# Loading x in two pairs of tiles, with both halves of the value weights between them

## The chip, the cores and the metric

The kernel runs on one core of one Trainium2 chip. The metric is the device time of one execution in microseconds (us), and the median of several executions is compared. The core has five engines that run side by side: TensorE (PE, matmuls; PEld is its weight load), VectorE (DVE), ScalarE (ACT), GpSimd (POOL) and SyncE (SP). Here SP does nothing but issue transfers from the chip's main memory into on-chip memory and back.

## The reference

The inputs are a sequence x of 2048 rows by 512, and weights, all in bfloat16. Two branches are computed from x and mixed row by row with a gate:

```
g = sigmoid((x * gate_w).sum(-1))
q, k, v = x @ wqkv, in 32 heads of 16
pq, pk = q @ w_phi, k @ w_phi               # per head
phi_q = [softmax(pq), softmax(-pq)];  phi_k likewise
kv = phi_k^T v;  z = sum of phi_k           # over all rows, per head
o = (phi_q kv) / (phi_q z + 1e-6);  a = o @ wo
b = relu(x @ w1) @ w2                        # inner width 1376
out = g * a + (1 - g) * b
```

## The kernel before

The 2048 rows are 16 tiles of 128, and four chunks of 512. On chip the kernel needs x with its columns on the partitions (`XT`), as the operand of every product with x. Chunks 1 to 3 come through transposing loads. The first chunk, tiles 0 to 3, is loaded as it is into part of the buffer `FT` and turned by TensorE: `xt{m}a` and `xt{m}b` are two matmuls each against an identity (line 321), for the first and second half of the columns of tile m. ScalarE copies the first half from the accumulator memory (PSUM) to `XT` (`xe{m}0`, line 333), VectorE the second (`xe{m}1`, line 335). "The turns" are these transposes.

Of the first chunk come then the value products `v{m}a`, `v{m}b` (line 369): two matmuls each of 128x512, with the first and second half of the value weights `WV`; ScalarE evicts the four-matmul result (`ve{m}`, line 374). The hidden units `h{c}_{k}` (line 392, four matmuls for chunk c and 128 of the inner columns) are evicted with a relu (`rl{c}_{k}`). The folds `f1_{j}` (line 351) multiply w_phi into the key weights, so that one product of x (`pr_k...`, line 449) gives pk; they need the key weights through the transposing load `wkT`, and are evicted as `fe1_{j}`, by VectorE for even j and ScalarE for odd j. All the rest of the kernel (softmax features, kv, the output products) comes behind.

PSUM has eight banks. The lines below give the transposes' banks, per tile for first and second half, and the folds' banks; the value tiles 0 to 3 accumulate in banks 2, 3, 4, 5 (`VB`), and the hidden units turn through 3, 4, 5 (`HB`):

```
XB, FB = ((0, 1), (6, 7), (0, 1), (6, 7)), (6, 7, 0, 1)
VB = (2, 3, 4, 5)
HB = (3, 4, 5)
```

The order of each engine's work is written out by name in the table `ORDER`, one list per engine, and each engine goes through its list in order. A task waits on semaphores for the tasks named in its dependencies; a load counts as done when it has landed whole. The numbers `dur` and `lat` in the source are a planner's costs and are not used when `ORDER` is given. SP's list starts with xa (three tiles of x, 384 KB), wva and wvb (the halves of the value weights, 256 KB each), xb (the fourth tile, 128 KB), then w1a (the first part of w1), wphi and wkT. In xa each partition holds three consecutive rows, so tile m of 0 to 2 holds rows 3p + m, and the function `rows` sends the output tiles back in the same manner.

While the first load is under way TensorE runs `warm0`, matmuls of constants whose result is not used (line 251).

Of the kernel before, what the change touches and what calls it, by code (L numbers as in the profile page):

```python
# [15 lines left out]

ORDER = {
    "sp": (
        "xa wva xb wvb w1a wphi wkT w1b x1 gw w1c wqT x2 x3 w2a ht0 w2b ht1 wo ht3 tq0 tq1 tq2 tq3 to0 to1 tq4 "
        "tq5 to2 to3 tq6 tq7 to4 ht2 to5 tq9 tq8 to6 to7 tq10 tq11 to8 to9 tq12 tq13 to10 to11 tq14 tq15 to12 "  # L20
        "to13 to14 to15 st15_1 "
    ),
# [6 lines left out]
    ),  # L29
    "act": (  # L30
# [20 lines left out]
    ),  # L51
# [29 lines left out]
class _Graph:  # L81
# [6 lines left out]
    def add(self, name, eng, fn, deps=(), dur=0.1, lat=None, dma=False):  # L88
        assert name not in self.tasks, name
        found = []  # L90
        for d in deps:
            if d is None:
                continue
            t = self.tasks[d]
            if t not in found:
                found.append(t)
        self.tasks[name] = _Task(name, eng, fn, found, dur, self.LAT[eng] if lat is None else lat, dma)
        return name
# [44 lines left out]
def bass_gated_mix__linear_kernel_hedgehog__dense_activation_relu__prompt_kernel(  # L143
# [11 lines left out]
    x2 = A_x.rearrange("b s d -> (b s) d")  # L155
    o2 = out.rearrange("b s d -> (b s) d")
    S, D = x2.shape
    H, DH = A_w_phi.shape[0], A_w_phi.shape[1]
    DFF = B_w1.shape[1]
    P = 128  # L160
# [13 lines left out]
    NPB, NTS, NF, NSL = 3, 3, 4, 3  # L174
# [6 lines left out]
    with ExitStack() as es:  # L181
        E = es.enter_context

        def sb(name, shape, dt):
            return E(nc.sbuf_tensor(name, shape, dt))
# [5 lines left out]
        WV = sb("WV", [P, ND, D], BF16)  # L191
# [8 lines left out]
        FT = sb("FT", [P, NF, 2 * F], BF16)  # L200
# [35 lines left out]
        add = g.add  # L236
# [12 lines left out]
        def pe_warm(q, sizes):  # L249
            for n in sizes:  # L250
                last = q.matmul(PS[:, 5, 0:n], ONE[:, 0:P], ONE[:, 0:n], start=True, stop=True)
            return last

        add("warm0", "pe", lambda q: pe_warm(q, (D, D, D, D, D, D, P, 2 * P)), (), dur=1.46)

        queue = {}

        def after_last(name, eng):
            if eng in queue:
                g.follow(queue[eng], name)  # L260
            queue[eng] = name

        def load(name, eng, out_, in_, deps=(), dur=0.1, lat=6.0, **how):
            add(name, eng, lambda q: q.dma_start(out=out_, in_=in_, **how), deps, dur=dur, lat=lat, dma=True)
            after_last(name, eng)
# [7 lines left out]

        w1r = B_w1.rearrange("(j p) n -> p j n", p=P)
        wvr = A_wqkv[:, 2 * D:3 * D].rearrange("(j p) n -> p j n", p=P)
        load("xa", "sp", FT[:, NF - 2, 0:3 * D], x2[0:3 * P, :].rearrange("(p t) d -> p (t d)", t=3), dur=0.47, lat=2.6)
        load("wva", "sp", WV[:, 0:2, :], wvr[:, 0:2, :], dur=0.47, lat=3.3)
        load("xb", "sp", FT[:, NF - 2, 3 * D:4 * D], x2[3 * P:4 * P, :], dur=0.47, lat=4.2)
        load("wvb", "sp", WV[:, 2:4, :], wvr[:, 2:4, :], dur=0.49, lat=3.8)
        load("w1a", "sp", W1[:, :, 0:512], w1r[:, :, 0:512], dur=0.5, lat=4.9)  # L280
        load("wphi", "sp", WPS[:, :, :], A_w_phi.rearrange("(g hl) r c -> (hl r) g c", g=ND), dur=0.55, lat=4.7)
        load_t("wkT", WT[:, ND:2 * ND, :], A_wqkv[:, D:2 * D], (), 4.55, 2.0)
# [25 lines left out]
        wbd = [f"wbd{j}" for j in range(ND)]  # L308


        def evict(name, eng, out_, b, deps):
            if eng == "act":
                add(name, eng, lambda q: q.activation(out_, PS[:, b, :], ACT.Copy), deps, dur=0.6)
            else:
                add(name, eng, lambda q: q.tensor_copy(out_, PS[:, b, :]), deps, dur=0.69)

        XB, FB = ((0, 1), (6, 7), (0, 1), (6, 7)), (6, 7, 0, 1)

        def pe_xt(q, m, n):
            for j in (2 * n, 2 * n + 1):  # L320
                last = q.matmul(PS[:, XB[m][n], (j % 2) * P:(j % 2 + 1) * P], XN[:, m, j * P:(j + 1) * P],  # L321
                                IDN[:, :], start=True, stop=True)
            return last

        for m in range(4):
            for n in range(2):
                add(f"xt{m}{'ab'[n]}", "pe", lambda q, m=m, n=n: pe_xt(q, m, n),
                    ("xa" if m < 3 else "xb", "ident", f"xe{m - 2}{n}" if m > 1 else None), dur=0.11)
            for n, eng in enumerate(("act", "dve")):
                xo = XT[:, 2 * n:2 * n + 2, m * P:(m + 1) * P]  # L330
                xi = PS[:, XB[m][n], 0:2 * P].rearrange("p (j t) -> p j t", j=2)
                if eng == "act":
                    add(f"xe{m}{n}", eng, lambda q, o=xo, i=xi: q.activation(o, i, ACT.Copy), (f"xt{m}a",), dur=0.38)
                else:
                    add(f"xe{m}{n}", eng, lambda q, o=xo, i=xi: q.tensor_copy(o, i), (f"xt{m}b",), dur=0.42)
# [6 lines left out]
        HB = (3, 4, 5)  # L342

        def rows(m):
            if m < 3:
                return o2[0:3 * P, :].rearrange("(p t) d -> p t d", t=3)[:, m, :]
            return o2[m * P:(m + 1) * P, :]

        def pe_fold(q, s, j, b):
            for i in range(ND):  # L350
                last = q.matmul(PS[:, b, i * P:(i + 1) * P], WT[:, s * ND + i, j * P:(j + 1) * P], WBD[:, i, :],  # L351
                                start=True, stop=True)
            return last

        for j in range(ND):
            b = FB[j]
            add(f"f1_{j}", "pe", lambda q, j=j, b=b: pe_fold(q, 1, j, b), ("wkT", *wbd, f"xe{3 - j // 2}{j % 2}"), dur=0.24)
            evict(f"fe1_{j}", ("dve", "act")[j % 2], WP[:, 1, j, :], b, (f"f1_{j}",))
        units = []
        for c in range(NC):  # L360
# [6 lines left out]
        def pe_v(q, m, js, b):  # L367
            for j in js:
                last = q.matmul(PS[:, b, :], XT[:, j, m * P:(m + 1) * P], WV[:, j, :],  # L369
                                start=(j == 0), stop=(j == ND - 1))  # L370
            return last

        def evict_v(m, b, deps):
            add(f"ve{m}", "act", lambda q: q.activation(  # L374
                ap(VS, NT * NG * GZ, m * NG * GZ, [[GZ, NG], [1, GV]]), psap(b * 512, [[GV, NG], [1, GV]]), ACT.Copy),
                deps, dur=0.6)

        for m in range(4):
            for n, js in enumerate(((0, 1), (2, 3))):
                add(f"v{m}{'ab'[n]}", "pe", lambda q, m=m, js=js: pe_v(q, m, js, VB[m]),  # L380
                    (f"xe{m}{n}", f"wv{'ab'[n]}", *((f"v{m}a",) if n else ())), dur=0.44)
            evict_v(m, VB[m], (f"v{m}b",))
        freed = {b: (f"ve{m}",) for m, b in enumerate(VB)}
        add("gt", "pe", lambda q: q.matmul(PS[:, 2, 0:ND], GWR[:, :], IDN[:, 0:ND], start=True, stop=True),  # L384
# [19 lines left out]
        n = 0  # L404
        for kind, a, k in units:
            b = HB[n % len(HB)]
# [23 lines left out]
        for c in range(NC):  # L430
# [3 lines left out]
                dur=0.2)  # L434
# [3 lines left out]
        for m in range(4, NT):  # L438
            add(f"v{m}", "pe", lambda q, m=m: pe_v(q, m, range(ND), 2), (*xof[m // 4], "wva", "wvb", f"ve{m - 1}" if m > 4 else "gv"),
                dur=0.865)  # L440
# [15 lines left out]
        for jn, (kind, tiles) in enumerate(jobs):  # L456
            w = len(tiles)
            n = kind_n[kind]
# [63 lines left out]
            else:  # L522
# [4 lines left out]
                    dur=0.11 + 0.207 * w)  # L527
# [24 lines left out]
                for m in tiles:  # L552
# [22 lines left out]
                    ab = HB[m % 3]  # L575
# [15 lines left out]
                    if m == NT - 1:  # L591
# [15 lines left out]
                        for h2 in range(2):  # L607
                            b, cs = hb[h2], cols[h2]
# [12 lines left out]
                            else:  # L621
                                add(f"oe{m}_1", "dve", lambda q, m=m, b=b, cs=cs: q.tensor_scalar(  # L622
                                    OSB[:, m % NOS, cs], PS[:, b, 0:cs.stop - cs.start], OMG[:, m:m + 1], None, ALU.mult), need,
                                    dur=0.4)
                            add(f"st{m}_{h2}", ("act", "sp")[h2], lambda q, m=m, cs=cs: q.dma_start(
                                out=o2[m * P:(m + 1) * P, cs], in_=OSB[:, m % NOS, cs]), (f"oe{m}_{h2}",), dur=0.5,
                                lat=1.5, dma=True)
# [5 lines left out]
                        (f"a{m}", f"go{m // 4}", f"st{m - NOS}" if m >= NOS else None), dur=0.69)  # L633
                    add(f"st{m}", "act", lambda q, m=m: q.dma_start(
                        out=rows(m), in_=OSB[:, m % NOS, :]), (f"oe{m}",), dur=0.39, lat=1.7, dma=True)

        for line in (("warm0", "xt0a", "xt0b", "xt1a", "xt1b", "xt2a", "xt2b", "xt3a", "xt3b", "h0_0"),
# [44 lines left out]
```

## Time and profile before

| | |
|---|---|
| median of 3 runs | 150.67 us (150.57 to 150.94) |
| the profiled execution | 150.76 us, of which the span from first to last instruction is 148.9 us |
| TensorE busy | 145.6 us, 98% |
| VectorE, GpSimd, ScalarE busy | 110.8, 109.6, 91.9 us |
| loads and stores | 16.11 MB moved, 108 GB/s in the mean |

The profile's times count from the start of the span. A line of the view in order of time has the start, the length, the engine, the line of the source, the operation, output and inputs, the number of instructions that were merged, and in brackets the idle time of that engine just before, with what ended it. PEld shows when weights are loaded, SPq when SP issues a transfer. The length of matmuls that follow each other includes the way through the array, so the pace is read from the starts.

### The profile page before, as it was taken

Reading aid. Unit: us, or ns where it says so; the run is one execution under the profiler, and the core shown is the slowest. Engines: PE = TensorE matmul, PEld = TensorE weight load, DVE = VectorE, ACT = ScalarE, POOL = GpSimd, SP = SyncE. Lnnn points to the kernel's source line nnn. Section 1 sums busy time; section 2 is a strip of 40 time slices with the busy share of each in tenths; the row PEclk is TensorE's granted clock in tenths of the full one; section 3 lists DMA queues with packets and bytes.
Section 4 is the critical chain, followed back from the end, with each engine's and each line's share of the span. In section 5 each row is a group of like instructions: output and inputs, shape, how many; then the busy total and the mean of one; then the engine's idle time right before and its main releaser. Section 6 shows DMA issues by size and latency. Waiting matters only on the chain.

```text
span 148.9 us, 2554 instructions
## 1 busy us (share of the span) xinstructions
PE 145.6 (98%) x984; PEld 73.6 (49%) x984; DVE 110.8 (74%) x169; ACT 91.9 (62%) x127; POOL 109.6 (74%) x73
## 2 busy tenths in 40 slices
PE   7999999999999999999999999999999999999994
PEld 2445444445446644455455545454545444445453
DVE  0344799999997769894879979799999966618301
ACT  3458679996896897774989591566455651303051
POOL 4000799999999999999999999999999924510000
DMA  4999999600200420000000135954767787864543
GB/s 148 292 179 236 238 176 237 221 0 0 65 1 0 97 88 0 0 0 0 4 2 0 35 70 135 116 135 112 170 48 174 184 206 144 174 146 116 128 151 101
DMA packets 45524, 16.11 MB, mean 108 GB/s; under 512 B 39272, under 2 KB 45384, under 8 KB 45512
## 3 DMA queue, kind: packets, MB, share of 16 engines
q1 hardware_dynamic: 43208, 13.89, 43.9%
q10 hardware_dynamic: 2304, 2.06, 4.3%
q8 instruction: 8, 0.13, 0.4%
q14 instruction: 4, 0.03, 0.1%
HBM read 4.41 MB, written 2.10 MB: 44 GB/s over the span
## 4 chain that ended last, share of the span: by engine, by line
PE 96%; DMA 2%; DVE 0%; issue 0%
PE PS L580 24%; PE PS L392 23%; PE PS L449 19%; PE PS L369 9%; PE PS L586 9%; PE PS L516 3%; PE PS L559 3%; DMA FT<-in_A_x_dram 2%; PE PS L400 2%; PE PS L601 2%; PE PS L351 1%; PE PS L321 1%; PE PS L612 1%; DVE OSB L622 0%; PE PS L384 0%
## 5 line engine op out<-in xcount | busy, mean ns | idle before, releaser
L495 POOL TENSOR_TENSOR TS<-MN,PB 128x1024 bf16<-128x1024 bf16 (+1 forms) x18 | 30.9, 1723 | 13.3 <-DVE MN L488 13.3
L392 PE MATMUL PS<-XT,W 128*128 128x512 bf16 x160 | 38.4, 379 | 0.0
L502 DVE TENSOR_REDUCE ZB<-FT 128x128 f32<-128x2048 bf16 (+1 forms) x18 | 36.5, 2031 | 1.9 <-ACT FT L500 1.8
L580 PE MATMUL PS<-W,HT 128*128 128x512 bf16 (+1 forms) x165 | 37.8, 379 | 0.0
L500 ACT ACTIVATE FT<-TS 128x2048 bf16<-128x2048 bf16 (+1 forms) x18 | 30.9, 1719 | 4.8 <-POOL TS L495 4.2
L495 POOL TENSOR_TENSOR TS<-PB,MX 128x1024 bf16<-128x1024 bf16 (+1 forms) x18 | 30.9, 1720 | 0.0
L449 PE MATMUL PS<-WP,XT 128*128 128x512 bf16 x128 | 30.1, 379 | 0.0
L509 POOL TENSOR_TENSOR FT<-FT,SC 128x2048 bf16<-128x2048 bf16 (+1 forms) x9 | 29.5, 3287 | 0.0
L410 ACT ACTIVATE HT<-PS 128x512 bf16<-128x512 f32 x40 | 22.6, 596 | 4.7 <-PE PS L392 3.9
L631 ACT ACTIVATE OSB<-PS,OMG 128x512 bf16<-128x512 f32 x15 | 10.3, 685 | 24.4 <-PE PS L586 24.3
L580 PEld LDWEIGHTS PS<-W,HT 128*128 128x128 bf16 (+1 forms) x165 | 15.4, 98 | 17.2 <-ACT OSB L631 0.7
L482 ACT ACTIVATE PB<-PS 128x1024 bf16<-128x1024 f32 (+1 forms) x18 | 16.7, 927 | 10.5 <-PE PS L449 5.5
L392 PEld LDWEIGHTS PS<-XT,W 128*128 128x128 bf16 x160 | 14.7, 98 | 16.4 <-ACT HT L410 0.9
L488 DVE TENSOR_REDUCE MN<-PB 128x64 bf16<-128x1024 bf16 (+1 forms) x18 | 19.4, 1090 | 4.4 <-ACT PB L482 4.3
L486 DVE TENSOR_REDUCE MX<-PB 128x64 bf16<-128x1024 bf16 (+1 forms) x18 | 19.4, 1086 | 3.6 <-ACT PB L482 3.6
L449 PEld LDWEIGHTS PS<-WP,XT 128*128 128x128 bf16 x128 | 12.2, 98 | 14.2 <-ACT PB L482 0.5
L369 PE MATMUL PS<-WV,XT 128*128 128x512 bf16 x64 | 16.4, 379 | 0.1
L532 POOL TENSOR_TENSOR FT<-FT,SR 128x1024 bf16<-128x1024 bf16 (+1 forms) x9 | 15.6, 1735 | 0.6
L586 PE MATMUL PS<-WO,OT 128*128 128x512 bf16 x60 | 14.8, 379 | 0.0
L567 DVE SCALAR_TENSOR_TENSOR OTM<-PS,EG,RD 128x256 bf16<-128x256 f32 x32 | 14.3, 467 | 0.2
L565 DVE RECIPROCAL RD<-PS 128x16 f32<-128x16 f32 x32 | 6.7, 234 | 8.8 <-PE PS L559 8.8
L374 ACT ACTIVATE VS<-PS 128x512 bf16<-128x512 f32 x16 | 9.4, 600 | 2.2 <-PE PS L369 2.2
(54 smaller groups left out, 98.2 us busy)
## 6 DMA issues: line engine op xcount, KB each, us to landing
out_dram<-OSB ACTq DMA_DIRECT2D x15, 128.0 KB, 2.2
W<-in_B_w_dram SPq DMA_DIRECT2D x1, 1280.0 KB, 7.3
W<-in_B_w_dram SPq DMA_DIRECT2D x2, 512.0 KB, 5.2
WV<-in_A_wqkv_dram SPq DMA_DIRECT2D x2, 256.0 KB, 4.1
WO<-in_A_wo_dram SPq DMA_DIRECT2D x1, 512.0 KB, 4.0
FT<-in_A_x_dram SPq DMA_DIRECT2D x1, 384.0 KB, 3.3
W<-in_B_w_dram SPq DMA_DIRECT2D x1, 352.0 KB, 3.8
PHQ<-FT SPq DMA_TRANSPOSE x16, 2.8
```

The lines of the kernel that those rows point to most:

```text
L369: last = q.matmul(PS[:, b, :], XT[:, j, m * P:(m + 1) * P], WV[:, j, :], start=(j == 0), stop=(j == ND - 1))
L392: last = q.matmul(PS[:, b, :], W1[:, j, k * P:(k + 1) * P], XT[:, j, chunk(c)], start=(j == 0), stop=(j == ND - 1))
L410: add(f"rl{a}_{k}", "act", lambda q, a=a, k=k, b=b: q.activation(HT[:, k, chunk(a)], PS[:, b, :], ACT.Relu), (f"h{a}_{k}",), dur=0.6)
L449: last = q.matmul(PS[:, pj + n, :], XT[:, j, m * P:(m + 1) * P], WP[:, s, j, :], start=(j == 2), stop=(j == 1))
L486: add(f"mx_{J}", "dve", lambda q, sl=sl, w=w, i=pbg: q.tensor_reduce(MX[:, sl, 0:w * H], i, AX.X, ALU.max), (f"ev_{J}", old("t1")), dur=0. ...
L488: add(f"mn_{J}", "dve", lambda q, sl=sl, w=w, i=pbg: q.tensor_reduce(MN[:, sl, 0:w * H], i, AX.X, ALU.min), (f"ev_{J}", old("t2")), dur=0. ...
L495: add(f"{tn}_{J}", "pool", lambda q, o3=o3, a3=a3, b3=b3: q.tensor_tensor(o3, a3, b3, ALU.subtract), (f"{'mx' if sg == 0 else 'mn'}_{J}", ...
L500: add(f"ex_{J}", "act", lambda q, fs=fs, ts=ts, w=w: q.activation(FT[:, fs, 0:w * F], TS[:, ts, 0:w * F], ACT.Exp), (f"t1_{J}", f"t2_{J}", ...
L502: add(f"sm_{J}", "dve", lambda q, fs=fs, sl=sl, w=w: q.tensor_reduce(ZB[:, sl, 0:2 * w * H], FT[:, fs, 0:w * F].rearrange("p (g d) -> p g ...
L509: add(f"nm_{J}", "pool", lambda q, f3=f3, sl=sl, w=w: q.tensor_tensor(f3, f3, SC[:, sl, 0:2 * w * H].unsqueeze(2).to_broadcast([P, 2 * w * ...
L580: last = q.matmul(PS[:, ab, :], HT[0:r, k, m * P:(m + 1) * P], W2[0:r, k, :], start=(k == 0), stop=False)
L586: last = q.matmul(PS[:, ab, :], OT[:, m % NOT, t, :], WO[:, t, :], start=False, stop=(t == ND - 1))
```

## The change

The first load takes two tiles of x and the second load of x the other two, each 256 KB, with two consecutive rows per partition; both halves of the value weights come between them. TensorE turns tiles 0 and 1, does all the value products of these two, and then turns tiles 2 and 3. Tile 2's transposes use banks 4 and 5, tile 3's banks 0 and 1; dependencies follow the banks. `v3a` waits for `xe21`, which frees bank 5. The warm-up has one matmul of 256 columns less. In ScalarE's list `ve1` comes ahead of `xe20`, and the orders of the first hidden units and folds and of their evictions change a little. The planner's costs in the loads change too.

```diff
 "sp":
-        "xa wva xb wvb w1a wphi wkT w1b x1 gw w1c wqT x2 x3 w2a ht0 w2b ht1 wo ht3 tq0 tq1 tq2 tq3 to0 to1 tq4 "
+        "xa wva wvb xb w1a wphi wkT w1b x1 gw w1c wqT x2 x3 w2a ht0 w2b ht1 wo ht3 tq0 tq1 tq2 tq3 to0 to1 tq4 "
 "act":
-        "xe00 xe10 xe20 xe30 ve2 ve0 ve1 ve3 fe1_3 rl0_1 fe1_1 rl0_0 ev_k0 rl0_2 ev_k1 ev_k2 ex_k0 rl0_3 rl0_5 "
+        "xe00 xe10 ve1 xe20 xe30 ve0 ve2 ve3 fe1_3 fe1_1 rl0_0 rl0_1 ev_k0 rl0_2 ev_k1 ev_k2 ex_k0 rl0_3 rl0_5 "
 "pe":
-        "warm0 xt0a xt0b xt1a xt1b xt2a xt2b v0a v2a v1a xt3a v1b v2b xt3b v0b v3a h0_1 v3b h0_0 f1_3 f1_2 f1_0 "
-        "f1_1 h0_2 pr_k0a pr_k0 pr_k1 pr_k2 pr_k3 h0_3 gt h0_5 h0_6 h0_4 h0_8 h0_9 v4 pr_k4 h1_0 h0_7 h1_1 pr_k5 "
+        "warm0 xt0a xt0b xt1a xt1b v0a v1a v1b v0b xt2a xt2b xt3a xt3b v2a v2b v3a h0_0 h0_1 v3b f1_3 f1_2 f1_1 "
+        "f1_0 h0_2 pr_k0a pr_k0 pr_k1 pr_k2 pr_k3 h0_3 gt h0_5 h0_6 h0_4 h0_8 h0_9 v4 pr_k4 h1_0 h0_7 h1_1 pr_k5 "
...
-        add("warm0", "pe", lambda q: pe_warm(q, (D, D, D, D, D, D, P, 2 * P)), (), dur=1.46)
+        add("warm0", "pe", lambda q: pe_warm(q, (D, D, D, D, D, D, P)), (), dur=1.36)
...
-        load("xa", "sp", FT[:, NF - 2, 0:3 * D], x2[0:3 * P, :].rearrange("(p t) d -> p (t d)", t=3), dur=0.47, lat=2.6)
-        load("wva", "sp", WV[:, 0:2, :], wvr[:, 0:2, :], dur=0.47, lat=3.3)
-        load("xb", "sp", FT[:, NF - 2, 3 * D:4 * D], x2[3 * P:4 * P, :], dur=0.47, lat=4.2)
-        load("wvb", "sp", WV[:, 2:4, :], wvr[:, 2:4, :], dur=0.49, lat=3.8)
+        def pair(i):
+            return x2[2 * i * P:2 * (i + 1) * P, :].rearrange("(p t) d -> p (t d)", t=2)
+
+        load("xa", "sp", FT[:, NF - 2, 0:2 * D], pair(0), dur=0.47, lat=2.35)
+        load("wva", "sp", WV[:, 0:2, :], wvr[:, 0:2, :], dur=0.47, lat=2.65)
+        load("wvb", "sp", WV[:, 2:4, :], wvr[:, 2:4, :], dur=0.48, lat=3.4)
+        load("xb", "sp", FT[:, NF - 2, 2 * D:4 * D], pair(1), dur=0.47, lat=3.9)
...
-        XB, FB = ((0, 1), (6, 7), (0, 1), (6, 7)), (6, 7, 0, 1)
+        XB, FB = ((0, 1), (6, 7), (4, 5), (0, 1)), (6, 7, 0, 1)
...
-                    ("xa" if m < 3 else "xb", "ident", f"xe{m - 2}{n}" if m > 1 else None), dur=0.11)
+                    ("xa" if m < 2 else "xb", "ident", f"xe0{n}" if m > 2 else None), dur=0.11)
...
-            if m < 3:
-                return o2[0:3 * P, :].rearrange("(p t) d -> p t d", t=3)[:, m, :]
+            if m < 4:
+                i = m // 2
+                return o2[2 * i * P:2 * (i + 1) * P, :].rearrange("(p t) d -> p t d", t=2)[:, m % 2, :]
...
-            add(f"f1_{j}", "pe", lambda q, j=j, b=b: pe_fold(q, 1, j, b), ("wkT", *wbd, f"xe{3 - j // 2}{j % 2}"), dur=0.24)
+            add(f"f1_{j}", "pe", lambda q, j=j, b=b: pe_fold(q, 1, j, b), ("wkT", *wbd, f"xe{(1, 3)[j // 2]}{j % 2}"), dur=0.24)
...
-                    (f"xe{m}{n}", f"wv{'ab'[n]}", *((f"v{m}a",) if n else ())), dur=0.44)
+                    (f"xe{m}{n}", f"wv{'ab'[n]}", f"v{m}a" if n else "xe21" if m == 3 else None), dur=0.44)
```

## The prediction

> **What bounds the kernel now.** I read the page first: the share of each engine, then the waits of TensorE. The span line and the engine line of the page:
>
> ```profile
> span 148.9 us, 2554 instructions
> ...
> PE 145.6 (98%) x984; PEld 73.6 (49%) x984; DVE 110.8 (74%) x169; ACT 91.9 (62%) x127; POOL 109.6 (74%) x73
> ```
>
> The list of waits, TensorE's own, over the whole span (us in total, times, longest):
>
> ```profile
> PE PS L251 <- PEq L667: 0.8, 1, 0.8
> PE PS L321 <- DMA FT<-in_A_x_dram: 0.3, 1, 0.3
> ```
>
> TensorE is the bound: 98% busy, and the only waits long enough to be listed are ahead of its first matmul and for the first load of x. From there a late or early TensorE stays late or early to the end. The order behind the folds (from h0_2 on) is untouched, so I compare one moment: the start of the first fold, f1_3. Ahead of it, before and after, stand the same 16 transposing matmuls, 16 value matmuls and 8 matmuls of two hidden units. TensorE in order of time (start, length, line):
>
> ```profile
> 0.77 3.04 PE L251 MATMUL PS<-const-bfloat16-1.0 128*128 128x512 bf16 x8 [0.77 <-PEq L667]
> 4.12 1.41 PE L321 MATMUL PS<-IDN,FT 128*128 128x128 bf16 x12 [0.31 <-DMA FT<-in_A_x_dram]
> 5.37 1.46 PE L369 MATMUL PS<-WV,XT 128*128 128x512 bf16 x6
> 6.67 0.27 PE L321 MATMUL PS<-IDN,FT 128*128 128x128 bf16 x2
> 7.00 1.02 PE L369 MATMUL PS<-WV,XT 128*128 128x512 bf16 x4
> ...
> 8.83 1.03 PE L392 MATMUL PS<-XT,W 128*128 128x512 bf16 x4
> 9.69 0.59 PE L369 MATMUL PS<-WV,XT 128*128 128x512 bf16 x2
> 10.12 1.03 PE L392 MATMUL PS<-XT,W 128*128 128x512 bf16 x4
> 10.99 1.06 PE L351 MATMUL PS<-WBD,WT 128*128 128x128 bf16 x16
> 11.88 1.03 PE L392 MATMUL PS<-XT,W 128*128 128x512 bf16 x4
> 12.74 1.46 PE L449 MATMUL PS<-WP,XT 128*128 128x512 bf16 x6
> ```
>
> The fold starts at 10.99. A full-width matmul costs 0.216 us of TensorE's time: 10.99 - 10.12 = 0.87 holds four, and so does 12.74 - 11.88 = 0.86. A narrow one costs 0.056: 11.88 - 10.99 = 0.89 holds sixteen. The twelve at 4.12 took far longer, 1.25 us up to 5.37: two reasons, seen in the weight loads.
>
> ```profile
> 4.52 0.25 PEld L321 LDWEIGHTS PS<-IDN,FT 128*128 128x128 bf16 x2
> 4.63 0.20 PEld L321 LDWEIGHTS PS<-IDN,FT 128*128 128x128 bf16 x2
> ...
> 4.99 0.37 PEld L321 LDWEIGHTS PS<-IDN,FT 128*128 128x128 bf16 x4 [0.16 <-ACT XT L333]
> ...
> 6.96 0.56 PEld L369 LDWEIGHTS PS<-WV,XT 128*128 128x128 bf16 x4 [0.20 <-issue]
> ```
>
> Narrow matmuls start 0.11 apart at 4.52 and 4.63: TensorE still runs at half pace there, and at full pace by 5.37, though the profile's clock (the 1.00) says the same throughout:
>
> ```profile
> 4.00:4.50 0.50, 0.38 (x4) 1.00 1.06 301
> ```
>
> At 4.99 xt2a waited until tile 0's copy had left banks 0 and 1. At 6.96 v1b had been held up 0.20: the landing rows below show the second half of the value weights (wvb) arriving just then.
>
> **The loads.** Issues of SP's queue, then time from issue to landing of xa, wva, xb, wvb and the transposing load wkT:
>
> ```profile
> 0.74 0.41 SPq L264 DMA_DIRECT2D FT<-in_A_x_dram  x1
> 1.20 0.42 SPq L264 DMA_DIRECT2D WV<-in_A_wqkv_dram  x1
> 1.67 0.46 SPq L264 DMA_DIRECT2D FT<-in_A_x_dram  x1
> 2.17 0.43 SPq L264 DMA_DIRECT2D WV<-in_A_wqkv_dram  x1
> ...
> 3.71 4.72 SPq L268 DMA_TRANSPOSE WT<-in_A_wqkv_dram  x1
> ```
>
> ```profile
> FT<-in_A_x_dram SPq DMA_DIRECT2D x1, 384.0 KB, 3.3
> WV<-in_A_wqkv_dram SPq DMA_DIRECT2D x1, 256.0 KB, 3.6
> FT<-in_A_x_dram SPq DMA_DIRECT2D x1, 128.0 KB, 3.4
> WV<-in_A_wqkv_dram SPq DMA_DIRECT2D x1, 256.0 KB, 4.7
> WT<-in_A_wqkv_dram SPq DMA_TRANSPOSE x1, 6.8
> ```
>
> So they land at 4.04, 4.80, 5.07, 6.87 and 10.51. Bytes go out in order of issue. The load queue in the stretches 2.5 to 3.5 and 3.5 to 4.5 us (packets, MB, share of 16 engines):
>
> ```profile
> q1 hardware_dynamic: 182, 0.36, 91.4%
> q1 hardware_dynamic: 351, 0.33, 108.5%
> ```
>
> Packets of about 2 KB (0.36 MB over 182) move 0.36/0.914 = 0.394 MB per fully used us; those of about 1 KB only 0.33/1.085 = 0.304.
>
> **xa is two tiles.** 256 KB for 384: 0.131 MB less, 0.33 us at 0.394. Ends: nothing, if latency alone sets it, and 0.43 at 0.304. I take 0.33, the rate of the stretch in which xa moves. xt0a starts at 4.12 - 0.33 = 3.79, and wva, second in line both times, lands at 4.47.
>
> **wvb and xb change places.** Ahead of and with the third load stand 768 KB as before, so wvb takes xb's landing, 5.07; its upper end is its own old delay, 1.67 + 4.7 = 6.37. xb, now fourth with 1 MB through as before, takes wvb's: 6.87. But its 256 KB go as 2 KB runs, 0.262 MB at 0.394 and not at 0.304: 0.66 for 0.86, so I take 6.87 - 0.20, rounded to 6.70. Ends: the other loads' 3.6 after issue, 2.17 + 3.6 = 5.77, and 6.87. The long one is nearer: same place, same bytes ahead. SP issues the same number of DMAs; w1a and all behind keep their places, each ahead of them still 1 MB.
>
> **The warm-up** loses its 256-column matmul:
>
> ```profile
> 3.39 0.42 PE L251 MATMUL PS<-const-bfloat16-1.0 128*128 128x256 bf16 x1
> ```
>
> It ends at 3.81, in the shadow of xa. Gone, it saves at most 3.81 - 3.79 = 0.02, and I count nothing; what its absence may do to TensorE's pace is a rival below.
>
> **The evictions** of the transposes, ScalarE's half with the value evictions and first fold eviction, then VectorE's half and its two fold evictions:
>
> ```profile
> 4.55 1.15 ACT L333 ACTIVATE XT<-PS 128x256 bf16<-128x256 f32 x3 [2.54 <-PE PS L321]
> 6.98 0.38 ACT L333 ACTIVATE XT<-PS 128x256 bf16<-128x256 f32 x1 [1.28 <-PE PS L321]
> ...
> 10.32 0.60 ACT L374 ACTIVATE VS<-PS 128x512 bf16<-128x512 f32 x1 [0.64 <-PE PS L369]
> 11.41 0.60 ACT L313 ACTIVATE WP<-PS 128x512 bf16<-128x512 f32 x1 [0.49 <-PE PS L351]
> ```
>
> ```profile
> 4.77 1.23 DVE L335 CAST XT<-PS 128x256 bf16<-128x256 f32 x3 [3.18 <-PE PS L321]
> 11.63 1.29 DVE L315 CAST WP<-PS 128x512 bf16<-128x512 f32 x2 [1.58 <-PE PS L351]
> ```
>
> A copy begins 0.43 after its transpose at half pace (4.55 - 4.12), 0.31 at full pace (6.98 - 6.67), takes 0.38, and TensorE goes on about 0.1 later, weight load included (4.93 to 4.99, then some 0.05).
>
> **The sum to the first fold.** xt0a 3.79; xe00 from 4.22 to 4.60; v0a at 4.70, wva being there since 4.47. Eight value matmuls (v0a v1a v1b v0b) x 0.216 = 1.73, to 6.43. What they need comes sooner: xe10 ends at 4.98, xe11 at 4.77 - 0.33 + 0.82 = 5.26, wvb lands at 5.07 against v1b's turn at 5.56. Then xt2a waits for xb: 6.70, with 0.05 to start 6.75, a stall of 0.32. The next seven narrow matmuls run to 7.20; v2a needs xe20: 6.75 + 0.31 + 0.38 + 0.1 = 7.55 rounded, a stall of 0.35 with nothing left to fill it. Then v2, v3, h0_0 and h0_1, 16 full matmuls x 0.216 = 3.46: the fold starts at 11.01, against 10.99. The change trades the earlier start (0.33) and the gone stalls on banks 0 and 1 and on wvb for two new ones of much the same size.
>
> **The small edits.** Tile 2's transposes in banks 4 and 5, tile 3's in 0 and 1: the new waits (xt3 on tile 0's copies, done by 4.9; v3a on xe21, done by about 7.7 against v3a's turn at 8.4) cost nothing. On ScalarE ve1 now stands ahead of xe20: v1b ends near 6.2, ve1 takes 0.60 to 6.8, and xe20 is not due until 7.06. v3b moves to the last place ahead of the folds, so ve3 (0.63 after v3b's start, as at 9.69 and 10.32) runs 11.21 to 11.81, then fe1_3 to 12.41 and fe1_1 to 13.01. The covers: h0_2, on ve3's bank, is due at 11.90 (spare 0.09); pr_k0a needs fe1_3 at 12.76; pr_k0 needs fe1_1 and, from VectorE, fe1_0 (12.94) at 13.19. If the cover of 0.09 fails, its excess is lost, no more. The swaps of the hidden units and of rl0_0 with rl0_1 cost nothing: h0_0 starts at 8.85, the first unit of before at 8.83, so w1a is as good as before. The two-row addressing of the stores keeps the number of stores; the last tile's is unchanged.
>
> The profiled execution took 150.76, its span 148.9 and 1.86 around it; the median of the runs is 150.67, 0.09 less. With +0.02: 150.76 + 0.02 - 0.09 = 150.69, forecast 150.7.
>
> **The rivals.** First, xb lands like the other loads (5.77): its stall of 0.32 goes, the second stall stays, the fold starts at 10.69, 0.30 sooner: 150.4. For it: three of four loads landed within 3.6. It cannot do much better: wkT lands at 10.51, its issue alone is 4.72 long and is not moved, so with 0.1 to start the fold comes no sooner than 10.6: a gain of 0.39 at most, 150.3, and over 0.45 only if wkT came sooner too.
>
> Second, slower: TensorE's full pace comes later. [...] Full-width matmuls then take twice 0.216; all eight of v0 and v1 at half pace end at 4.70 + 3.46 = 8.16, not 6.43. xb's stall absorbs 0.32; the rest, 1.41, is lost: 152.1. It decides from about four slow matmuls on (0.86 - 0.32 = 0.54). [...]
>
> Third, slower: wvb keeps its old delay and lands at 6.37. v1b waits from 5.56, v1b and v0b end at 7.28, ve1 holds ScalarE to about 7.6 ahead of xe20, v2a starts near 8.1: the fold comes 0.55 later, 151.2. For it: something delayed wvb and not xb in the trace; against it, by bytes the place in the queue explains it. Beside it, xb one us later than its place: 151.7.
>
> **How the numbers follow.** About 0.3% (0.45 us) is what a measurement of this kernel can tell from no change: below 150.22 or above 151.12. Chances: the sum 0.48, at 150.7 with 150.5 to 150.9; xb early 0.24, at 150.4, of which 0.10 below 150.22; late pace 0.11; wvb late 0.12, of which half inside 0.3%; xb later still 0.05. Of the sum's own 0.48, 0.03 on either side for what it misses: faster 0.10 + 0.03 = 0.13; slower 0.11 + 0.06 + 0.05 + 0.03 = 0.25; same the other 0.62. The range 150.2 to 151.3 takes in both ends of xb and the late wvb, and leaves out late pace, the latest xb and the far end of the gain, about 0.2.
>
> **What would show it.** First transpose near 3.79; v0a near 4.70; wvb landing near 5.07 with no wait at v1b; xt2a waiting for x near 6.7; a wait on ScalarE's copy ahead of v2a, near 7.55; first fold near 11.0, and from there the old distances. It is wrong if TensorE's value matmuls at 4.7 to 6.4 run 0.43 apart, if wvb lands past 5.6, or if the fold's moment does not carry to the end.

## The result and the profile after

The changed kernel takes 151.07 us in the median of 20 runs (150.44 to 152.27), the kernel before 150.66 (150.26 to 151.13): a ratio of 1.0031, with a 95% interval of 1.0019 to 1.0044. It is slower by about 0.3%, 0.4 to 0.5 us.

The profiled execution is not a typical one: it took 150.47, the second shortest of the 20, with a span of 148.5 against 148.9 before. Its TensorE in order of time (start, length, line; lines 321, 369, 392, 449 and 351 of before are 324, 373, 396, 453 and 355 here):

```profile
0.77 2.82 PE L251 MATMUL PS<-const-bfloat16-1.0 128*128 128x512 bf16 x7 [0.77 <-PEq L671]
3.59 1.03 PE L324 MATMUL PS<-IDN,FT 128*128 128x128 bf16 x8
4.46 2.09 PE L373 MATMUL PS<-WV,XT 128*128 128x512 bf16 x8
6.39 0.61 PE L324 MATMUL PS<-IDN,FT 128*128 128x128 bf16 x8
7.14 1.47 PE L373 MATMUL PS<-WV,XT 128*128 128x512 bf16 x6
8.45 1.89 PE L396 MATMUL PS<-XT,W 128*128 128x512 bf16 x8
10.17 0.59 PE L373 MATMUL PS<-WV,XT 128*128 128x512 bf16 x2
10.60 1.06 PE L355 MATMUL PS<-WBD,WT 128*128 128x128 bf16 x16
```

and the landings, from issue, of wva, wvb and xb:

```profile
WV<-in_A_wqkv_dram SPq DMA_DIRECT2D x1, 256.0 KB, 3.0
WV<-in_A_wqkv_dram SPq DMA_DIRECT2D x1, 256.0 KB, 3.3
FT<-in_A_x_dram SPq DMA_DIRECT2D x1, 256.0 KB, 3.8
```

Here everything landed early. The eight value matmuls of tiles 0 and 1 run without waiting for a load from 4.46 to xt2a at 6.39, xb (issued at 2.18) is in by 6.0, only the stall on xe20 is left (the last of eight turns starts at 6.78, v2a at 7.14), and the first fold comes at 10.60, 0.39 sooner than the 10.99 of before. The span is shorter by as much (0.4). Against this one profile of before the change wins; but the kernel before also has runs of 150.26, below the shortest of the changed kernel, 150.44. What the other runs lose is not in this trace, and the first experiment looks for it.

### The profile page after: what moved, and what is told of

It is laid out like the page before. It is cut to its first block, busy times and chain, and to the rows that moved or that the text cites. A ratio compares the mean times of both kernels' runs of the same rounds, so it can differ in the third digit from the quotient of the medians.

```text
span 148.5 us, 2536 instructions
## 1 busy us (share of the span) xinstructions
PE 144.5 (97%) x966; PEld 73.5 (50%) x983; DVE 110.9 (75%) x169; ACT 91.7 (62%) x127; POOL 109.6 (74%) x73
## 4 chain that ended last, share of the span: by engine, by line
PE 95%; ACT 2%; issue 1%; DVE 1%
PE PS L584 24%; PE PS L396 23%; PE PS L453 18%; PE PS L373 9%; PE PS L590 8%; PE PS L563 3%; PE PS L520 3%; PE PS L251 2%; PE PS L605 2%; PE PS L404 1%; PE PS L355 1%; ACT VS L378 1%; PE PS L324 1%; PE PS L616 1%; ACT PB L486 0%
## 5 line engine op out<-in xcount | busy, mean ns | idle before, releaser
L396 PE MATMUL PS<-XT,W 128*128 128x512 bf16 x156 | 37.7, 379 | 0.2
L584 PE MATMUL PS<-W,HT 128*128 128x512 bf16 (+1 forms) x161 | 37.1, 379 | 0.2
L453 PE MATMUL PS<-WP,XT 128*128 128x512 bf16 x123 | 29.6, 379 | 0.3
```

The lines of the kernel that those rows point to most:

```text
L396: last = q.matmul(PS[:, b, :], W1[:, j, k * P:(k + 1) * P], XT[:, j, chunk(c)], start=(j == 0), stop=(j == ND - 1))
L453: last = q.matmul(PS[:, pj + n, :], XT[:, j, m * P:(m + 1) * P], WP[:, s, j, :], start=(j == 2), stop=(j == 1))
L584: last = q.matmul(PS[:, ab, :], HT[0:r, k, m * P:(m + 1) * P], W2[0:r, k, :], start=(k == 0), stop=False)
```

## The experiments

Two theories stood at the start. The landing theory (the first expectations call it the loads theory): in most runs wvb, xb or xa lands later, and TensorE, which works in the written order, stands still. The pace theory, a supposition: the shorter warm-up and the new pauses (the first ahead of v0a) delay TensorE's full pace. Ratios are to the kernel before, run beside it on the same chip. The runs were made on three chips, on which the kernel before had medians of 150.42 to 150.66, so runs are compared by their ratios and not by their medians; a ratio need not be that of the two medians. In brackets stands its 95% interval. Moments without a row beside them are starts of single matmuls and landings in the same traces.

**The same kernel again**, for a second profile.

> The changed kernel as it is, for a second profile: the first profiled execution took 150.47, far below the median of 151.07, so the place of the usual 0.6 us is not in it. Loads theory: xb (or xa) lands later than in the first profile (6.0 and 3.5), the stall ahead of xt2a grows by 0.3 to 0.8, and the full-width matmuls run 0.22 apart by 5.4. Pace theory: the loads land as before, but full-width matmuls still run 0.43 apart past 5.4, some 2 to 4 of them more than in the first profile, for 0.4 to 0.8 us. Median by both: 150.9 to 151.2.

151.14 us, ratio 1.0034 [1.0018, 1.0050]; the profiled execution took 151.33. TensorE in order of time, and the landings of wvb and xb:

```profile
3.63 0.81 PE L324 MATMUL PS<-IDN,FT 128*128 128x128 bf16 x8
4.50 1.04 PE L373 MATMUL PS<-WV,XT 128*128 128x512 bf16 x4
5.95 1.02 PE L373 MATMUL PS<-WV,XT 128*128 128x512 bf16 x4 [0.41 <-DMA WV<-in_A_wqkv_dram]
7.28 0.62 PE L324 MATMUL PS<-IDN,FT 128*128 128x128 bf16 x8 [0.30 <-DMA FT<-in_A_x_dram]
8.04 1.47 PE L373 MATMUL PS<-WV,XT 128*128 128x512 bf16 x6
9.34 1.89 PE L396 MATMUL PS<-XT,W 128*128 128x512 bf16 x8
11.07 0.59 PE L373 MATMUL PS<-WV,XT 128*128 128x512 bf16 x2
11.50 1.06 PE L355 MATMUL PS<-WBD,WT 128*128 128x128 bf16 x16
```

```profile
WV<-in_A_wqkv_dram SPq DMA_DIRECT2D x1, 256.0 KB, 4.1
FT<-in_A_x_dram SPq DMA_DIRECT2D x1, 256.0 KB, 5.1
```

This execution is the longest of its ten (150.77 to 151.33), so it shows the loss at its largest. The idle times in brackets count from the modelled end of a matmul; by the starts, v0a and v1a are done by 5.37 (4.50 + 4 x 0.216) and v1b starts at 5.95, 0.58 late, with wvb landing at 5.8. The next four full matmuls end at 6.81, and xt2a starts at 7.28, 0.47 late, on xb. Both waits are there, 1.05 us, and the fold comes 0.90 later than in the first profile. They don't count alike: xt2a needs xb as well as the end of v0b. Had wvb been in time, v0b would have ended near 6.23 (4.50 + 8 x 0.216), and xt2a would still have waited for xb until 7.28. The wait that decides here is xb's. The pace theory already fails here: the four full matmuls from 4.50 take 1.04 in all, which is 0.22 apart, so the full pace came earlier than in the first profile, whose eight turns took 1.03 against 0.81.

The rest of the span is the same: 148.5 - 10.60 = 137.9, 149.4 - 11.50 = 137.9, before 148.9 - 10.99 = 137.9, and 137.9 to 138.1 in all later profiles. What happens ahead of the first fold is nearly the whole difference.

**The warm-up given back.**

```diff
-        add("warm0", "pe", lambda q: pe_warm(q, (D, D, D, D, D, D, P)), (), dur=1.36)
+        add("warm0", "pe", lambda q: pe_warm(q, (D, D, D, D, D, D, P, 2 * P)), (), dur=1.46)
```

> One part undone: the warm-up has its 256-column matmul again. Pace theory: the shorter warm-up is what delays the full pace, so the time goes back by most of the 0.4 us, to about 150.6. Loads theory: no change against the changed kernel beyond 0.15 us, 151.0; if xa lands before 3.8 it can even cost up to 0.2.

151.04 us, ratio 1.0038 [1.0023, 1.0053]: nothing came back. Its profiled execution (151.02) lies at the median, unlike the two profiles so far:

```profile
4.50 1.04 PE L373 MATMUL PS<-WV,XT 128*128 128x512 bf16 x4
5.98 1.02 PE L373 MATMUL PS<-WV,XT 128*128 128x512 bf16 x4 [0.44 <-DMA WV<-in_A_wqkv_dram]
6.84 0.61 PE L324 MATMUL PS<-IDN,FT 128*128 128x128 bf16 x8
```

v1b waits for wvb again, from 5.37 to 5.98, but xt2a follows v0b without a break, as xb had landed at 6.50. Here wvb's wait is the one that decides.

**The kernel before with the shorter warm-up** (the same line the other way round).

> One part alone: the kernel before with the shorter warm-up. Pace theory: slower by 0.3 to 0.5 us, about 151.0. Loads theory: no change, 150.66 within 0.15.

150.45 us, ratio 0.9992 [0.9971, 1.0012]: no change. In its profile two value matmuls run at half pace (starts 5.21, 5.63, 5.96, then 0.22 apart), which costs little, since wvb lands only at 6.66 there. With these two runs the shorter warm-up is out as the cause of the loss; the new pauses are out by the profiles, which show TensorE at full pace at v0a and late all the same.

**Work behind xt2b.** v0b moved so that TensorE has something to do while tile 2 is copied.

```diff
-        "... v0a v1a v1b v0b xt2a xt2b xt3a xt3b v2a ..."
+        "... v0a v1a v1b xt2a xt2b v0b xt3a xt3b v2a ..."
```

> The changed kernel with v0b moved behind xt2b, so that TensorE has two value matmuls to do while tile 2 is copied. Loads theory: where xb is on time the stall ahead of v2a (0.36 in the first profile) shrinks to under 0.1, 0.25 us faster; where xb is late v0b waits behind it and nothing is won; median 150.8 to 151.0. Pace theory: the full 0.3 us in every execution, about 150.75.

151.23 us, ratio 1.0032 [1.0013, 1.0050]: nothing won, a miss for the 150.8 to 151.0 I gave it. Its profile:

```profile
3.65 0.62 PE L324 MATMUL PS<-IDN,FT 128*128 128x128 bf16 x8
4.42 1.04 PE L373 MATMUL PS<-WV,XT 128*128 128x512 bf16 x4
6.40 0.59 PE L373 MATMUL PS<-WV,XT 128*128 128x512 bf16 x2 [0.95 <-DMA WV<-in_A_wqkv_dram]
6.98 0.40 PE L324 MATMUL PS<-IDN,FT 128*128 128x128 bf16 x4
7.21 0.59 PE L373 MATMUL PS<-WV,XT 128*128 128x512 bf16 x2
7.64 0.39 PE L324 MATMUL PS<-IDN,FT 128*128 128x128 bf16 x4
7.96 1.47 PE L373 MATMUL PS<-WV,XT 128*128 128x512 bf16 x6
```

Here TensorE ran at full pace from its first transpose (eight in 0.62, first start to last end) and had all it wanted until 5.3, and then stood more than a microsecond at v1b. The stall on xe20 is filled, but v0b now stands behind the wait for xb and no longer in front of it.

**No wait for wvb.** v0b and v1b use the first half of the value weights, so that tiles 0 and 1 of v are computed from the wrong half; wvb is still loaded.

```diff
-                last = q.matmul(PS[:, b, :], XT[:, j, m * P:(m + 1) * P], WV[:, j, :],
+                last = q.matmul(PS[:, b, :], XT[:, j, m * P:(m + 1) * P], WV[:, j % 2 if m < 2 else j, :],
...
-                    (f"xe{m}{n}", f"wv{'ab'[n]}", f"v{m}a" if n else "xe21" if m == 3 else None), dur=0.44)
+                    (f"xe{m}{n}", f"wv{'ab'[n if m > 1 else 0]}", f"v{m}a" if n else "xe21" if m == 3 else None), dur=0.44)
```

> The changed kernel, but v0b and v1b use the first half of the value weights in place of the second (so tiles 0 and 1 of v are computed from the wrong half of the weights), and so don't wait for wvb, which is still loaded. Landing theory (wvb, third, often lands near 5.8 to 6.3 and TensorE stands at v1b with nothing else to do): v0b ends near 6.2, xt2a waits for xb alone, the first fold comes 0.3 to 0.5 us sooner, median 150.6 to 150.8. Rival (the wait at v1b only hides the wait for xb, which lands near 6.5 to 7.2 anyway): under 0.15 us sooner, 151.0.

150.93 us, ratio 1.0017 [1.0002, 1.0033]: about half of the loss went, less than I gave it. Its profiled execution is the shortest of the twelve (150.51) and shows no wait for a load behind xa: xb landed at 6.31 and v0b ended at 6.51. So the half that is left is in no trace of this run.

**No wait for xb alone**: tiles 2 and 3 are turned from the rows of tiles 0 and 1.

```diff
-                last = q.matmul(..., XN[:, m, j * P:(j + 1) * P],
+                last = q.matmul(..., XN[:, m % 2, j * P:(j + 1) * P],
...
-                    ("xa" if m < 2 else "xb", "ident", ...
+                    ("xa", "ident", ...
...
-                war += [f"xt{m}b" for m in range(4)]
+                war += [*(f"xt{m}b" for m in range(4)), "xb"]
```

The last edit only keeps a later task from writing into the buffer before xb has landed.

> The changed kernel, but tiles 2 and 3 are turned from the rows of tiles 0 and 1 (so half of the first chunk is computed from the wrong rows) and xb, still loaded, isn't waited for; the wait for wvb stays. Taking away both waits gave back all of the 0.3%, taking away wvb's about half. Landing theory: this gives back the other part, ratio to the kernel before 1.001 to 1.002 (150.6 to 150.9). Rival (xb's wait is all in the shadow of wvb's): no different from the changed kernel, 1.003.

150.92 us, ratio 1.0031 [1.0015, 1.0048]: no different from the changed kernel, the rival's number. In its profile v1b stood until wvb came, at 6.20, and v0b ended at 7.19, when xb too had landed (6.89):

```profile
6.33 1.02 PE L373 MATMUL PS<-WV,XT 128*128 128x512 bf16 x4 [0.95 <-DMA WV<-in_A_wqkv_dram]
```

**No wait for either**, both edits together.

> As the one before, and tiles 2 and 3 are turned from the rows of tiles 0 and 1 (so they are computed from the wrong rows), so that xb isn't waited for either; both loads are still made. Landing theory: TensorE goes from 4.5 to the fold with only the stall on xe20, is ready for it near 10.4 and then waits for wkT (10.5 to 10.9): 150.1 to 150.4, at or below the kernel before. Rival for what is left (the order itself, the shorter warm-up, the evictions): 150.8 or more.

150.77 us, ratio 1.0001 [0.9984, 1.0019]: the loss is gone. Alone among the three runs that leave out a wait, its interval ends where the changed kernel's begins; the other two overlap with it, and for them the ratios themselves are all there is. But nothing is won over the kernel before, as the 150.1 to 150.4 would have had it. TensorE in its profile, with the load of its weights for the fold, and the landings of w1a and wkT:

```profile
6.94 1.47 PE L373 MATMUL PS<-WV,XT 128*128 128x512 bf16 x6
8.75 1.89 PE L396 MATMUL PS<-XT,W 128*128 128x512 bf16 x8 [0.34 <-DMA W<-in_B_w_dram]
10.47 0.59 PE L373 MATMUL PS<-WV,XT 128*128 128x512 bf16 x2
```

```profile
10.82 0.96 PEld L355 LDWEIGHTS PS<-WBD,WT 128*128 128x128 bf16 x16 [0.25 <-DMA WT<-in_A_wqkv_dram]
```

```profile
W<-in_B_w_dram SPq DMA_DIRECT2D x1, 512.0 KB, 5.9
WT<-in_A_wqkv_dram SPq DMA_TRANSPOSE x1, 7.1
```

The next loads are the new bound. The first hidden unit was due at 8.24 (6.94 + 6 x 0.216) and starts at 8.75, 0.5 late, since w1a (issued at 2.69) landed at 8.6. The fold, at 10.90, then follows v3b without a break: wkT, at 10.8, has just come. Without the wait for w1a the fold would have been due at 10.4 and would have waited for wkT. So leaving out both waits takes the whole 0.3% away, as far as the intervals tell, and each wait lies for the most part in the other's shadow: xt2a starts when the later of xb and v0b is there, and which of them that is changes from run to run (xb in the second profile, v0b behind wvb in the one with the warm-up given back).

**wvb last, xb third**, TensorE turning tiles 2 and 3 and doing v2a, v3a before the first product that needs wvb.

```diff
-        "xa wva wvb xb w1a ..."
+        "xa wva xb wvb w1a ..."
...
-        "xe00 xe10 ve1 xe20 xe30 ve0 ve2 ..."
+        "xe00 xe10 xe20 xe30 ve1 ve0 ve2 ..."
...
-        "... v0a v1a v1b v0b xt2a xt2b xt3a xt3b v2a v2b v3a h0_0 h0_1 v3b ..."
+        "... v0a v1a xt2a xt2b xt3a xt3b v2a v3a v1b v0b v2b h0_0 h0_1 v3b ..."
```

> The pairs of tiles are kept, but wvb is fourth again and xb third, and TensorE turns tiles 2 and 3 and does v2a and v3a before the first product that needs wvb (v1b). Landing theory: one exposed wait (xt2a for the third load) in place of two; the last landing is covered by v2a and v3a; the fold near 10.9 to 11.1, 150.5 to 150.8. Rival (it is not the places of the waits): 151.0 to 151.2 as the changed kernel.

151.10 us, ratio 1.0017 [1.0000, 1.0034]. The median is a miss, the ratio lies between the two theories, and its interval reaches to both. In the profile, the longest of its twelve executions (151.41), the third load, now xb, landed 4.6 after its issue, and TensorE stood from 5.3 to 6.37 in its place:

```profile
6.37 0.62 PE L324 MATMUL PS<-IDN,FT 128*128 128x128 bf16 x8 [0.95 <-DMA FT<-in_A_x_dram]
```

In this execution, then, xb is exposed in third place as wvb was: it is not the value weights as such that are slow.

**Only the two loads change places**, in the kernel before with its three tiles in xa.

```diff
-        "xa wva xb wvb w1a ..."
+        "xa wva wvb xb w1a ..."
```

> One part alone: the kernel before, three tiles in xa and its own order on TensorE, with only wvb and xb changing places in SP's queue. Landing theory: it is not the order of the loads but the work at hand while they are out; with three tiles in xa, six value matmuls that need only xa and wva run from about 5.3 to 6.6, and both the third and the fourth load land mostly under them: ratio to the kernel before within 0.0015 of 1. Rival (the place in the queue decides, whatever TensorE has to do): slower by 0.3%, as the changed kernel.

150.49 us, ratio 0.9998 [0.9977, 1.0018]. wvb landed 4.3 after its issue at 1.67, near 6.0, no sooner than in the changed kernel, and TensorE did not wait for it:

```profile
WV<-in_A_wqkv_dram SPq DMA_DIRECT2D x1, 256.0 KB, 4.3
```

```profile
3.70 1.41 PE L321 MATMUL PS<-IDN,FT 128*128 128x128 bf16 x12
4.95 1.53 PE L369 MATMUL PS<-WV,XT 128*128 128x512 bf16 x6
6.34 0.28 PE L321 MATMUL PS<-IDN,FT 128*128 128x128 bf16 x2
6.47 1.03 PE L369 MATMUL PS<-WV,XT 128*128 128x512 bf16 x4
```

From 4.95 to 6.34 TensorE works on six value matmuls that need xa and wva only. With two tiles there are four, and they end at 5.2 to 5.4. That is what the change gave away.

**What delays the third load?** Two trials. First the transposing load wkT, issued behind w1b and w1c, which now go out ahead of it (I took this for 1.0 us later; it was 1.5):

> The changed kernel with the transposing load wkT issued behind w1b and w1c, 1.0 us later, to see what delays the third and fourth load. The time is worse by about 1 us, since the folds wait for wkT (near 11.7 to 12), that is not the question. If the transposing load disturbs the loads in flight: wvb lands by 5.1 and xb by 6.1, as in the first profile. If not: wvb 5.6 to 6.3 and xb 6.5 to 7.2, as in the later ones.

153.15 us. wvb landed 4.5 after its issue, as late as ever, though wkT went out at 5.24 and not at 3.71: in this one profile wkT's early issue is not what delays wvb. (w1b and w1c went out in its place, at 3.71, so the queue was not empty.) The time is worse by more than the 1 us I gave, as the fold waited for wkT until 13.36. Then the load of w_phi, with its many short runs (512 packets of 32 bytes in the first profile's trace), taken from SP to ScalarE's queue:

> The changed kernel with the load of w_phi, many short runs, taken out of SP's queue and issued by ScalarE behind xe10 (near 5 us); wkT goes out 0.55 us sooner. Theory that w_phi's load is what delays single engines near 4 us: wvb lands by 5.1 and xb by 6.1, and the median falls to about 150.6. Theory that the late landings come from the large loads themselves: wvb lands at 5.3 to 6.3 as before, median 150.9 to 151.2.

152.11 us. wvb landed 4.4 after its issue. This does not clear w_phi wholly, since it still went out at 4.33; the time is worse because it landed late, and its own users with it:

```profile
12.46 1.05 PE L355 MATMUL PS<-WBD,WT 128*128 128x128 bf16 x16 [0.57 <-DVE WBD L308]
```

**All four tiles in the first load**, then wva and wvb, eight value matmuls that need wva alone ahead of the others, and a warm-up that reaches to xa.

```diff
-        "xa wva wvb xb w1a ..."
+        "xa wva wvb w1a ..."
...
-        "xe00 xe10 ve1 xe20 xe30 ve0 ve2 ..."
+        "xe00 xe10 xe20 xe30 ve1 ve2 ve0 ..."
...
-        "warm0 xt0a xt0b xt1a xt1b v0a v1a v1b v0b xt2a xt2b xt3a xt3b v2a v2b v3a h0_0 h0_1 v3b ..."
+        "warm0 xt0a xt0b xt1a xt1b xt2a xt2b xt3a xt3b v0a v1a v2a v3a v1b v2b v0b v3b h0_0 h0_1 ..."
...
-        add("warm0", "pe", lambda q: pe_warm(q, (D, D, D, D, D, D, P)), (), dur=1.36)
+        add("warm0", "pe", lambda q: pe_warm(q, (D, D, D, D, D, D, D, 2 * P)), (), dur=1.36)
```

> All four tiles in the first load (512 KB, four rows per partition), then wva and wvb; the eight value matmuls that need only wva come ahead of those that need wvb, the warm-up is longer to reach xa. One issue less on SP. Landing theory: xa lands near 4.4, the first value matmul near 5.4, 1.7 us of value products cover wvb until 7.1, and no later wait is exposed: the fold near 10.6, 150.2 to 150.4, faster than both kernels. Rival (late starts can't be made up): xa later than 4.6 or a stall among the turns, the fold near 11, 150.7.

150.66 us, ratio 0.9999 [0.9976, 1.0022]: the kernel before's time, not the 150.2 to 150.4 expected. The first part went as expected (xt0a at 4.24, the first value matmul at 5.28), but in the profiled run wvb landed 5.9 after its issue, near 7.6, past even the eight matmuls of cover (the value products are line 368 here):

```profile
5.28 1.89 PE L368 MATMUL PS<-WV,XT 128*128 128x512 bf16 x8
7.64 1.90 PE L368 MATMUL PS<-WV,XT 128*128 128x512 bf16 x8 [0.48 <-DMA WV<-in_A_wqkv_dram]
```

With xa at 512 KB, 1 MB goes out up to the end of this third load, as up to the fourth of the changed kernel, and 7.6 is about where the latest of those landed (2.17 + 5.3). No version beat the kernel before: the ratios of 0.9992 and 0.9998 above have 1 well inside their intervals.

## Why the prediction was right and wrong

The forecast was 150.7 with no change beyond 0.3% as likeliest; measured are 151.07 and +0.31% [+0.19, +0.44]. The range of 150.2 to 151.3 held it, but the likeliest case was not the one that happened. The nearest is the third rival, wvb late, 151.2, with its number met partly by luck: TensorE started 0.2 sooner than forecast, which hid part of the loss, and in the second profile xb, 0.5 later than forecast, was as much to blame as wvb.

- **The bound and the carrying to the end** were right: from the fold on, every profile has 137.9 to 138.1 us.
- **xa and wva** were right in kind and somewhat better than forecast: first transpose at 3.59 and 3.63 against 3.79, v0a at 4.46 and 4.50 against 4.70. Against the profile of before (4.12) the start is 0.5 us sooner, not 0.33; but that moves too: with 384 KB in xa the run with the two loads exchanged started at 3.70.
- **wvb at 5.07: this step failed**, by the sign that the prediction itself names ("if wvb lands past 5.6"). "wvb takes xb's landing, 5.07" held in the first profile (1.67 + 3.3 = 4.97). In the nine profiles with the changed kernel's order of loads wvb landed at 4.97 to 6.26, in the middle at 5.89. In ten of the eleven later profiles with a load of 256 KB in third place it landed 3.7 to 4.6 after its issue, in the other 5.9; the 3.4 that I carried over belonged to a load of 128 KB in one execution. By the prediction's own rates wvb should have been put 0.10 later than that, since of the 768 KB ahead of and with it 0.131 MB now go as 1 KB runs and no longer as xa's longer ones (0.131/0.304 - 0.131/0.394); that is small beside the 0.8 measured. The upper end I gave, 6.37, was near the usual case and should not have had a chance of 0.12.
- **xb at 6.70** was a little early: in the same nine profiles it landed at 6.00 to 7.45, in the middle at 6.89. The 0.20 taken off for the longer runs is 0.10 by the prediction's own rates, as the shorter xa has the opposite effect ahead of it.
- **What the two do together**: v1b and v0b take 0.86 us and start about 0.1 behind wvb. With wvb at 5.89 they end near 6.9, when xb has landed too. So xt2a starts at 7.28 in the second profile and at 6.84 with the warm-up given back, in place of the 6.75 of the sum, once by xb and once by wvb.
- **The cover of wvb** was where the exposure could have been read. I compared landings with v1b's turn, and not the work at hand: before, six matmuls ran without wvb, after the change four. The trace of before shows a short wait at v1b (0.20) with wvb landing at 6.87; with less work ahead of v1b, a landing near 6 costs most of a microsecond there.
- **The stall on xe20** (0.35) was right: in the first profile the last turn starts at 6.78 and takes 0.06, and v2a starts at 7.14, a stall of 0.30. **ve1 ahead of xe20** cost nothing, as said: in the first profile xe20 starts 0.31 after xt2a.
- **The warm-up**, counted at nothing: right, by two runs (ratios of 1.0038 with it given back, 0.9992 with the shorter one in the kernel before). **The late pace** happened only in small: the eight value matmuls from 4.46 took 2.09 in the first profile, where eight at full pace take 1.89, as one ran at half pace; in the profiles above that stood at v1b TensorE was at full pace from v0a on. The latest full pace in any profile is that with w_phi on ScalarE's queue, with four value matmuls at half pace (starts 4.34, 4.74, 5.17, 5.59), all ahead of its wait for wvb. Half pace through all eight, the 152.1 case, is shown by no run; it was the author's estimate.
- **The cap by wkT** is there, but not alone and not at a fixed moment. In the run without both waits w1a, which the prediction took to be as good as before, holds TensorE first, and wkT comes just in time for the fold that this leaves (10.8 for 10.90). wkT's issue on SP took 4.72 before, 3.78 in the first profile and 5.00 in that run, so the bound itself moves from run to run.

## What to carry to other kernels

Where an engine works in a fixed order, a load is covered by the work that stands ahead of its first user and needs nothing later; count that work in matmuls before and after, and set it against the spread of the landing, not against one landing. The smaller first load brought the start forward here by 0.1 to 0.5 us (first transpose at 3.59, against 3.70 with the two loads exchanged and 4.12 before), but took from the loads behind it work that covered them: the earlier start was paid for with two exposed waits. Where two waits follow each other, what one is worth is read from which of them ends last; here leaving out one wait gave ratios of 1.0017 and 1.0031, leaving out both 1.0001. One profile of a kernel can be its best run or its worst; compare its time with the median before reading it.

## What the runs showed of the hardware

The landing in a row is the last of a load's 16 completion marks: 1.67 + 3.3 is the 4.97 of the first line below, and 1.67 + 4.1 and 1.67 + 4.5 come to the 5.81 and 6.20 of the others within the rounding. The marks of the third load in three traces, us from the start of the span, the 16 in order:

```
first profile     4.79 4.80 4.81 4.82 4.83 4.84 4.85 4.86 4.87 4.88 4.89 4.90 4.91 4.92 4.94 4.97
second profile    4.64 4.65 4.66 4.68 4.72 4.88 4.92 4.94 5.02 5.06 5.07 5.11 5.31 5.52 5.65 5.81
no wait for xb    4.32 4.33 4.34 4.44 4.60 4.62 4.68 4.70 4.75 4.78 4.79 5.04 5.07 5.10 5.14 6.20
```

The middle ones stand at 4.7 to 5.0 in all three; the last comes 0.1 to 1.5 later. In the second and third trace v1b started at 5.95 and 6.33, 0.14 and 0.13 behind the last mark. What holds up single marks stays open: with wkT moved wvb still landed 4.5 after its issue, and moving w_phi's load (4.4) was no clean trial.

TensorE's full pace comes at a different moment from run to run. The same eight transposes, started at 3.59, 3.63 and 3.65, took 1.03, 0.81 and 0.62 us. In the last case the pace was full 2.9 us behind the first matmul (3.65 - 0.77). What sets the moment stays open.
